# A mixture-of-experts kernel behind attention: units of 512 tokens in place of units of 256

## The chip, the cores and the metric

The kernel runs on one core of one Trainium2 chip. The metric is the device time of one execution in microseconds (us). Engines are named as the profile names them: PE is TensorE (PEld its weight loads), DVE is VectorE, ACT is ScalarE, POOL is GpSimd and SP is SyncE, which only issues transfers here.

## What is computed

The reference is sparse attention followed by a top-1 mixture of experts. Attention has 4 batches, 8 heads, 768 positions and 64 columns a head; a position sees the 96 before it and 8 global ones, with a linear bias on distance. Its rows (3072 x 512) go through a gate, and each token through the one expert that wins:

```python
    logits = x @ w_gate + modality_bias[modality_id]
    e_idx = np.argmax(logits, axis=1)
    # probs: softmax of logits; gate_w: the winner's probability
    for e in range(E):                                  # E = 8
        mask = e_idx == e
        h = np.maximum(x[mask] @ w1[e], 0.0)            # 512 -> 1024
        out[mask] = gate_w[mask, None] * (h @ w2[e])    # 1024 -> 512
```

How many tokens an expert gets is known only on the chip. With the inputs that are timed, experts 0, 3 and 5 get 1567, 1406 and 99 tokens, the others none.

## The kernel before

**Attention** is 24 steps of 128 rows, issued by `step(n)`: scores of block n on PE (L209), a maximum per row on DVE (L224, `mx`), exponentials on ACT (L240), four transposes for each of three PSUM banks (`t_mm`, L254), a copy of each bank to SBUF (`t_cp`), and the product with the values for block n - 2 (`pv`, L279 and L290). `t_cp(n, x, act)` puts a copy on ACT (L261) or on DVE (L263); the middle one of the three is DVE's, except in the last step. Behind the values come the row sums' reciprocal, the scaled rows (`xr`, L321), their transposes and copy (L335, L337), and the gate. When all six blocks of a batch have their gates, tokens are ranked by expert: matmuls `pk` (L409, L410) count them, a DVE copy (L419) takes the counts, and a scatter writes token numbers to `ids_sorted`. For three of the four batches that falls into steps 10, 16 and 22.

**Experts** follow, and three early units begin while the last batch is still ranked: 256 tokens each, of experts that the first two batches have filled (e0, e1, e2). Everything else waits for a plan that DVE works out on the chip in arrays of expert by item (`items`, `slots`, `granules`): 8 units of 256 (s0 to s7) and granules of up to 128 tokens (g0, g1), the last a small one of up to 32 rows beside the final unit (g2). The order of the slots is e0, e1, e2, s0, s1, g0, s2, s3, g1, s4 to s7. The plan's instructions come from a generator, `rest()`, that `fill(u, k)` advances once for each of 16 parts of an early unit; so they stand between that unit's own instructions on DVE.

A slot loads 4 MB of weights. fp32 accuracy comes from splitting each operand into a high part, cast by ACT (L665 for weights, L680 for tokens), and the rest, subtracted by DVE (L666, L681), and from three matmuls for each product. `l1_unit` has weights stationary and 256 tokens moving: 96 matmuls of 256 columns (L694 to L696), two of the eight feature blocks in one PSUM bank, then ReLU on ACT (L700) and the subtraction on DVE (L701) 512 wide. `l2` has tokens stationary: 48 matmuls of 512 columns (L736 to L738), into one bank `po` for each 128 tokens. `fin` scales a bank into SBUF on ACT (L805) and POOL scatters the rows (L806). `x_t` transposes the next slot's tokens late in a slot, four transposes and one ACT and one DVE instruction for each 128 tokens.

**What sets the order.** PE and ACT run in the order that the program writes. The scheduler interleaves DVE's instructions. SP works in order, and a load of token numbers or weights first reads a register from the plan's result. Each `po` comes from a pool of two banks, so a bank must be emptied by ACT before it is filled again.

## Time and profile before

| what | value |
|---|---|
| runs | 448.81, 448.84, 450.58 us; median 448.84 us |
| profiled execution | 451.22 us, of which the span on the core is 449.3 us |
| busy | PE 429.9 us (96%), DVE 300.9 (67%), ACT 274.5 (61%), POOL 111.4 (25%) |
| mean granted TensorE clock | 0.992 of full speed |
| bytes moved | 110.24 MB at a mean of 245 GB/s |
| attention | from the first scores at 5.4 us until about 143 us |
| experts | from there to about 437.7 us, PE busy throughout |

Busy time counts from an instruction's start to its end, and matmuls overlap, so the distance between the starts of two is what a matmul costs in a full stream. "Idle before <- releaser" in a row names what ended a wait. The rest of the span, from 437.7 to 449.3 us, is the last scatter and its landing.

### The profile page before, as it was taken

How to read it: one execution, taken by the hardware profiler on the slowest of the kernel's cores; microseconds unless marked ns; L12 is line 12 of the kernel's file. 1: busy time of each engine (PE TensorE's matmuls, PEld its weight loads, DVE VectorE, ACT ScalarE, POOL GpSimd, SP SyncE). 2: the span in 40 equal slices, each digit the busy share in tenths (PEclk: the TensorE clock that was granted, in tenths of full speed). 3: DMA queues.
4: the chain of work that ended last, by engine and by line, in shares of the span. 5: the costliest groups of instructions: out<-in, count | busy, mean ns of one | idle time of the engine just before them, and what ended most of it. 6: DMA issues, size and time to landing. Idle time of an engine off the chain costs nothing.

```text
span 449.3 us, 12795 instructions
## 1 busy us (share of the span) xinstructions
PE 429.9 (96%) x4872; PEld 378.8 (84%) x4872; DVE 300.9 (67%) x945; ACT 274.5 (61%) x508; POOL 111.4 (25%) x173
## 2 busy tenths in 40 slices
PE   7999998989999999999999999999999999999990
PEld 7889887878887989889898988989889898989860
DVE  7878786778778678898374786574956746465500
ACT  5988887877877263645554677454864645554420
POOL 6010013122423257340404053021123030301010
PEclk9999999999999999999999999999999999999996
DMA  8999999987867658485848488675797666565510
GB/s 238 323 332 329 343 366 332 276 249 249 290 214 251 231 174 348 154 288 204 306 157 302 165 310 303 231 258 210 242 364 255 226 229 215 185 211 208 187 34 27
DMA packets 58197, 110.24 MB, mean 245 GB/s; under 512 B 8575, under 2 KB 22399, under 8 KB 58128
## 3 DMA queue, kind: packets, MB, share of 16 engines
q1 hardware_dynamic: 53456, 96.49, 64.4%
q0 software_dynamic: 4672, 12.85, 7.8%
q8 instruction: 40, 0.66, 0.6%
q14 instruction: 29, 0.24, 0.1%
HBM read 94.95 MB, written 14.43 MB: 243 GB/s over the span
## 4 chain that ended last, share of the span: by engine, by line
PE 75%; issue 13%; DVE 3%; ACT 3%; DMA 2%; POOL 2%; POOLq 0%; SPq 0%; DVEq 0%; ACTq 0%
PE s L209 6%; PE pt L254 6%; PE phs L696 5%; PE phs L694 5%; PE phs L695 5%; PE x L290 5%; PE pos L738 4%; PE pos L737 4%; PE pos L736 4%; PE phe L694 3%; PE phe L696 3%; PE phe L695 3%; PE poe L738 2%; PE poe L736 2%; PE poe L737 2%
## 5 line engine op out<-in xcount | busy, mean ns | idle before, releaser
L240 ACT ACTIVATE pr<-sc,nmx 128x168 f32<-128x168 f32 x192 | 67.6, 425 | 13.3 <-DVE nmx L224 10.7
L696 PE MATMUL phs<-xhs,als 128*128 128x256 f32 x256 | 72.4, 283 | 0.0
L694 PE MATMUL phs<-xhs,ahs 128*128 128x256 f32 x256 | 72.3, 282 | 0.0
L695 PE MATMUL phs<-xls,ahs 128*128 128x256 f32 x256 | 72.2, 282 | 0.0
L224 DVE CUSTOM_DVE_ANT_0 sc<-s,tbl 128x168 f32<-128x168 f32 x192 | 52.7, 329 | 15.0 <-PE s L209 13.4
L701 DVE SCALAR_TENSOR_TENSOR hls<-phs,hhs 128x512 fp32r<-128x512 f32 x32 | 22.1, 692 | 51.1 <-ACT hhs L700 48.5
L618 POOL DMA_INDIRECT xgs<-x_rows,uis x16 | 24.0, 1501 | 119.6 <-DMA uis<-ids_sorted 56.7
L736 PE MATMUL pos<-bhs,hhs 128*128 128x512 f32 x128 | 52.0, 406 | 0.0
L738 PE MATMUL pos<-bhs,hls 128*128 128x512 f32 x128 | 50.6, 396 | 0.0
L737 PE MATMUL pos<-bls,hhs 128*128 128x512 f32 x128 | 50.5, 394 | 0.0
L694 PEld LDWEIGHTS phs<-xhs,ahs 128*128 128x128 f32 x256 | 48.9, 191 | 0.4
L700 ACT ACTIVATE hhs<-phs 128x512 fp32r<-128x512 f32 x32 | 19.1, 598 | 49.2 <-PE phs L696 38.5
L695 PEld LDWEIGHTS phs<-xls,ahs 128*128 128x128 f32 x256 | 48.9, 191 | 0.3
L696 PEld LDWEIGHTS phs<-xhs,als 128*128 128x128 f32 x256 | 48.9, 191 | 0.1
L209 PE MATMUL s<-kt,qt 64*64 64x168 f32 x768 | 38.0, 312 | 2.7 <-DVE nmx L224 1.9
L445 POOL DMA_INDIRECT ids_sorted<-tki,pi x24 | 26.5, 1103 | 43.6 <-ACT pr L240 31.0
L254 PE MATMUL pt<-ident,pr 128*128 128x128 f32 x288 | 36.7, 277 | 0.0
L209 PEld LDWEIGHTS s<-kt,qt 64*64 64x64 f32 x768 | 29.6, 132 | 7.5 <-DVE nmx L224 3.7
L254 PEld LDWEIGHTS pt<-ident,pr 128*128 128x128 f32 x288 | 31.0, 141 | 4.5 <-issue 3.2
L261 ACT COPY pT<-pt 128x512 f32<-128x512 f32 x49 | 28.3, 587 | 6.7 <-PE pt L254 5.0
L736 PEld LDWEIGHTS pos<-bhs,hhs 128*128 128x128 f32 x128 | 24.1, 189 | 6.7 <-issue 2.1
L806 POOL DMA_INDIRECT out<-obs,ois x16 | 16.6, 1037 | 52.7 <-ACT obs L805 50.2
(346 smaller groups left out, 999.9 us busy)
## 6 DMA issues: line engine op xcount, KB each, us to landing
va<-in_vr SPq DMA_DIRECT2D x24, 520.0 KB
kt<-in_ks SPq DMA_DIRECT2D x24, 272.0 KB
qt<-in_qs SPq DMA_DIRECT2D x24, 256.0 KB
x_rows<-xr SPq DMA_DIRECT2D x24, 256.0 KB
vl<-in_vo SPq DMA_DIRECT2D x48, 81.2 KB
rawe0a<-in_moe_w SPq DMA_DIRECT2D x4, 512.0 KB
rawe0b<-in_moe_w SPq DMA_DIRECT2D x4, 512.0 KB
rawe1a<-in_moe_w SPq DMA_DIRECT2D x4, 512.0 KB
```

Source lines behind the costliest of these rows:

```text
L209: nc.tensor.matmul(ps[g][64 * half : 64 * half + 64, c0 : c0 + W], qt[hs, hp, 64 * half : 64 * half + 64], kt[hs, hp, w0 : w0 + W], start= ...
L224: V.tensor_tensor_reduce(out=sc, in0=pss[n][g][:, c0 : c0 + W], in1=(tbl0 if n % NB == 0 else tbl)[:, hh, :], op0=ALU.add, op1=ALU.min, sc ...
L240: last[0] = nc.scalar.activation(pr[:, h * (PRW - W) : h * (PRW - W) + W], scs.pop((n, hh)), AF.Exp, bias=blk[n][:, hh : hh + 1], scale=-1.0,)
L254: nc.tensor.transpose(tp[:, j * P : (j + 1) * P], prs[(NP * n + hp) % NPR][:, o : o + P], ident)
L261: last[0] = nc.scalar.copy(pT.rearrange("p a b -> p (a b)"), tp)
L445: ins = nc.gpsimd.indirect_dma_start(out=ids, out_offset=bass.IndirectOffsetOnAxis(ap=pi[:, j : j + 1], axis=0), in_=tki[:, b * NB + j, :] ...
L694: nc.tensor.matmul(o, hi[:, fs], s.xh[:, c, :], start=(c == 0), stop=False)
L695: nc.tensor.matmul(o, hi[:, fs], s.xl[:, c, :], start=False, stop=False)
L696: nc.tensor.matmul(o, lo[:, fs], s.xh[:, c, :], start=False, stop=(c == 3))
L736: nc.tensor.matmul(s.po[t], s.hh[:, fc, tt], hi[:, wv], start=(fc == 0), stop=False)
L737: nc.tensor.matmul(s.po[t], s.hh[:, fc, tt], lo[:, wv], start=False, stop=False)
L738: nc.tensor.matmul(s.po[t], s.hl[:, fc, tt], hi[:, wv], start=False, stop=(fc == 7))
```

## The change

The tokens that the early units leave are taken in three *duos* of 512 tokens (`halves` = 4, named b0 to b2), two units of 256 (c0, c1) and the same granules. With the inputs that are timed the plan makes duos of (expert 0, tokens 768 to 1279), (3, 0 to 511) and (3, 512 to 1023), units of (0, 1280 to 1535) and (3, 1024 to 1279), and granules of 126, 99 and 31 tokens, which are the tokens of the 8 units and 3 granules before. The order is e0, e1, e2, b0, g0, b1, g1, c0, b2, c1, with g2 beside the last. There are 11 slots that load weights where there were 14.

- `l1_duo` makes one PSUM bank from a feature block and 512 moving tokens: 96 matmuls, and two ReLUs and two subtractions 256 wide for each of the 8 blocks.
- The second layer of a duo is two passes over the same weights, tokens 0 to 255 and then 256 to 511. Between them `fin(s, [0, 1])` empties the two banks.
- The plan sorts items into duos, odd units and rests. `granules` looks at four thresholds in place of two, over 32 places in place of 16, and the generator is advanced twice for a part of an early unit, except in the first unit's first parts.
- The split b weights have one buffer in place of two. A duo's further tiles come from a new pool, `mp2`. A granule's b split is written at parts 17, 19, 21 and 23 of a duo. Transposes of the next slot's tokens are up to four.
- In the attention, `t_cp` of the middle bank goes to ACT in three more steps: 10, 16 and 17.

```diff
@@ -35,13 +35,14 @@
 U = 256
 NE = 3
 BE = 2
-NS = 8
+ND = 3
+NS = 5
 NGR = 3
 NGF = 2
 MR = 32
 NI = 17
-NR = NI - NS
-NGT = 16
+NR = NI - ND
+NGT = 32
...
-ORDER = (0, 1, 8, 2, 3, 9, 4, 5, 6, 7, 10)
-TX = (11, 12)
-TB = (7, 9, 11, 13)
+ORDER = (0, 5, 1, 6, 3, 2, 4, 7)
+TB = (17, 19, 21, 23)
...
+        units, full = pl("units", [E]), pl("full", [E])
         V.tensor_scalar(ci, ci, 8, None, ALU.logical_shift_right)
+        V.tensor_copy(units, ci)
+        V.tensor_scalar(ci, ci, 1, None, ALU.logical_shift_right)
         V.tensor_copy(full, ci)
+        odd = pl("odd", [E])
+        V.scalar_tensor_tensor(odd, full, -2.0, units, ALU.mult, ALU.add)
...
+        V.tensor_tensor(m3, bm(sin, ni), uc, ALU.is_gt)
+        V.tensor_tensor(w, bm(sex, ni), uc, ALU.is_gt)
+        V.tensor_sub(m3, m3, w)
+        V.tensor_tensor(w, m3, bm(full, ni), ALU.mult)
+        V.tensor_add(st, st, w)
...
-        h1 = pl("h1", [NR])
-        V.tensor_scalar(h1, nr, 0.0, None, ALU.is_gt)
-        h2 = pl("h2", [NR])
-        V.tensor_scalar(h2, nr, 128.0, None, ALU.is_gt)
-        m = pl("m", [1])
-        V.reduce_sum(m, h1, axis=AX.X)
-        m2 = pl("m2", [1])
-        V.reduce_sum(m2, h2, axis=AX.X)
...
+        lt = pl("lt", [NR, NR])
+        V.tensor_tensor(lt, bc(uidx[:, 0:NR], NR), bm(uidx[:, 0:NR], NR), ALU.is_gt)
+        m, m2 = pl("m", [1]), pl("m2", [1])
+        V.memset(m, 0.0)
+        sa, sk, wr, wk = pl("sa", [NGT, NR]), pl("sk", [NGT, NR]), pl("wr", [NGT]), pl("wk", [NGT])
+        hk, pk, w1_ = pl("hk", [NR]), pl("pk", [NR]), pl("w1", [NR, NR])
         gi = uidx[:, 0:NGT]
-        gm = pl("gm", [NGT])
-        V.tensor_scalar(gm, gi, m, None, ALU.subtract)
-        s1 = pl("s1", [NGT, NR])
-        behind(V.tensor_tensor(s1, bc(gi, NR), bm(uidx[:, 0:NR], NGT), ALU.is_equal), last[0])
-        V.tensor_tensor(s1, s1, bm(h1, NGT), ALU.mult)
-        s2 = pl("s2", [NGT, NR])
-        V.tensor_tensor(s2, bc(gm, NR), bm(uidx[:, 0:NR], NGT), ALU.is_equal)
-        V.tensor_tensor(s2, s2, bm(h2, NGT), ALU.mult)
         yield
+        for k in range(4):
+            V.tensor_scalar(hk, nr, 128.0 * k, None, ALU.is_gt)
+            V.tensor_tensor(w1_, lt, bm(hk, NR), ALU.mult)
+            V.reduce_sum(pk, w1_, axis=AX.X)
+            V.tensor_scalar(pk, pk, m, 1.0, ALU.add, ALU.add)
...
+            t = sk if k else sa
+            V.tensor_tensor(t, bc(gi, NR), bm(pk, NGT), ALU.is_equal)
+            if k:
+                V.reduce_sum(wk, sk, axis=AX.X)
+                if k == 1:
+                    V.tensor_copy(wr, wk)
+                else:
+                    V.scalar_tensor_tensor(wr, wk, float(k), wr, ALU.mult, ALU.add)
+                V.tensor_add(sa, sa, sk)
...
-        nb = 2 if which == "b" and s.straight else 1
         pool = wspb if which == "b" or early else wsp
-        th = pool.tile([P, 1024], F32R, tag=f"{which}h{c}{early}", name=f"{which}h{s.name}{c}", bufs=nb)
-        tl = pool.tile([P, 1024], F32R, tag=f"{which}l{c}{early}", name=f"{which}l{s.name}{c}", bufs=nb)
+        th = pool.tile([P, 1024], F32R, tag=f"{which}h{c}{early}", name=f"{which}h{s.name}{c}", bufs=1)
+        tl = pool.tile([P, 1024], F32R, tag=f"{which}l{c}{early}", name=f"{which}l{s.name}{c}", bufs=1)
...
+            pool, w = (mp2, 2 * U) if s.halves == 4 else (mp, U)
+            s.xh = pool.tile([P, 4, w], F32R, tag="xh", name=f"xh{s.name}")
+            s.xl = pool.tile([P, 4, w], F32R, tag="xl", name=f"xl{s.name}")
...
+        if s.halves == 4:
+            s.hh2 = mp2.tile([P, 8, U], F32R, tag="hh", name=f"hh{s.name}b")
+            s.hl2 = mp2.tile([P, 8, U], F32R, tag="hl", name=f"hl{s.name}b")
+
+    def l1_duo(s, f):
+        ph = p_t(f"ph{s.name}{f}")
+        fs = slice(f * P, (f + 1) * P)
+        for c in range(4):
+            hi, lo = s.hi["a", c], s.lo["a", c]
+            nc.tensor.matmul(ph, hi[:, fs], s.xh[:, c, :], start=(c == 0), stop=False)
+            nc.tensor.matmul(ph, hi[:, fs], s.xl[:, c, :], start=False, stop=False)
+            nc.tensor.matmul(ph, lo[:, fs], s.xh[:, c, :], start=False, stop=(c == 3))
+        for hh, hl, o in ((s.hh, s.hl, 0), (s.hh2, s.hl2, U)):
+            last[0] = nc.scalar.activation(hh[:, f, :], ph[:, o : o + U], AF.Relu)
+            V.scalar_tensor_tensor(
+                hl[:, f, :], ph[:, o : o + U], 0.0, hh[:, f, :].bitcast(F32), ALU.max, ALU.subtract
+            )
...
-        if fc == 0 and not s.po:
-            s.po = {t: p_x(f"po{s.name}{t}") for t in range(2)}
+        if fc == 0 and t not in s.po:
+            s.po[t] = p_x(f"po{s.name}{t}")
         hi, lo = s.hi["b", fc // 2], s.lo["b", fc // 2]
         wv = slice(fc % 2 * 512, fc % 2 * 512 + 512)
-        tt = slice(t * P, (t + 1) * P)
-        nc.tensor.matmul(s.po[t], s.hh[:, fc, tt], hi[:, wv], start=(fc == 0), stop=False)
-        nc.tensor.matmul(s.po[t], s.hh[:, fc, tt], lo[:, wv], start=False, stop=False)
-        nc.tensor.matmul(s.po[t], s.hl[:, fc, tt], hi[:, wv], start=False, stop=(fc == 7))
+        tt = slice(t % 2 * P, (t % 2 + 1) * P)
+        hh, hl = (s.hh2, s.hl2) if t > 1 else (s.hh, s.hl)
+        nc.tensor.matmul(s.po[t], hh[:, fc, tt], hi[:, wv], start=(fc == 0), stop=False)
+        nc.tensor.matmul(s.po[t], hh[:, fc, tt], lo[:, wv], start=False, stop=False)
+        nc.tensor.matmul(s.po[t], hl[:, fc, tt], hi[:, wv], start=False, stop=(fc == 7))
...
-            t_cp(n - 1, 1, n == LAST)
+            t_cp(n - 1, 1, n in (NB + 4, 2 * NB + 4, LAST - 1, LAST))
...
-        uei, uoi, inv = slots("b", plan, *[t[:, 0:NS] for t in r], NS, 2)
-        for u in range(NS):
-            slist.append(mk(f"s{u}", uei[0:1, u : u + 1], uoi[0:1, u : u + 1], inv[:, :, u], xd, 2))
-        yield
+        for tag, u0, u1, hv in (("b", 0, ND, 4), ("c", ND, NS, 2)):
+            uei, uoi, inv = slots(tag, plan, *[t[:, u0:u1] for t in r], u1 - u0, hv)
+            for u in range(u1 - u0):
+                slist.append(mk(f"{tag}{u}", uei[0:1, u : u + 1], uoi[0:1, u : u + 1], inv[:, :, u], xd, hv))
+            yield
...
+    mp2 = sM.enter_context(tc.tile_pool(name="mp2", bufs=1, side="right", reuse_waits="tile"))
     man = tc.manual_schedule(engines={ET.Activation})
     man.__enter__()
     bg = rest()
@@ -1394,6 +1436,8 @@
         s = order[u]
         if u < NE:
             next(bg, None)
+            if u or k > 8:
+                next(bg, None)
...
-        if nx.halves == 1 and k in TB:
+        if nx.halves == 1 and s.halves == 4 and k in TB:
             split(nx, "b", TB.index(k))
-        if k >= 8 and k % 2 == 0:
+        if 8 <= k < 16 and k % 2 == 0:
             if ("a", k // 2 - 4) in nx.raw:
                 split(nx, "a", k // 2 - 4)
-        if s.halves == 2 and k in TX:
-            x_t(nx, TX.index(k))
+        if s.halves > 1:
+            x0 = (23 if s.halves == 4 else 15) - 2 - max(nx.halves, 2)
+            if x0 <= k < x0 + nx.halves:
+                x_t(nx, k - x0)
...
-        for m in range(0 if u else LF, 16):
-            if m >= 8:
+        for m in range(0 if u else LF, 24 if s.halves == 4 else 16):
+            if m >= 8 and s.halves == 4:
+                for t in (0, 1):
+                    l2(s, (m - 8) % 8, m // 16 * 2 + t)
+                if m == 15:
+                    fin(s, [0, 1])
...
+            elif s.halves == 4:
+                l1_duo(s, m)
...
-            if s.halves == 1 and m in (7, 10) and u + 1 < nslot:
-                x_t(order[u + 1], m // 10)
-        if u + 1 < nslot:
+            if s.halves == 1 and m in (7, 9, 10, 12) and u + 1 < nslot:
+                ts = (7, 10) if order[u + 1].halves == 2 else (7, 9, 10, 12)
+                if m in ts:
+                    x_t(order[u + 1], ts.index(m))
+        if s.halves == 4:
+            fin(s, [2, 3])
```

The listing of instructions in each engine's order shows three places. The first is on PE at the end of the second layer. `pos` and `pob` are the PSUM banks `po` of a unit and of a duo, `hhs` and `hhb` the hidden activations, `bhs` and `bhb` the b weights, `phs` the next slot's first layer. Before, at the end of the first unit of the plan:

```order
L736 MATMUL pos_4821<-bhs_4816,hhs_4656 128x512
L737 MATMUL pos_4821<-bls_4817,hhs_4656 128x512
L738 MATMUL pos_4821<-bhs_4816,hls_4657 128x512
L694 MATMUL phs_4916<-xhs_4854,ahs_4828 128x256 [waits Activation_49]
L695 MATMUL phs_4916<-xls_4855,ahs_4828 128x256 [waits DVE_49]
L696 MATMUL phs_4916<-xhs_4854,als_4829 128x256
```

Now, between the two passes of the first duo:

```order
L776 MATMUL pob_4950<-bhb_4942,hhb_4748 128x512
L777 MATMUL pob_4950<-blb_4943,hhb_4748 128x512
L778 MATMUL pob_4950<-bhb_4942,hlb_4749 128x512
L776 MATMUL pob_5024<-bhb_4828,hhb0b 128x512 [waits Activation_49]
L777 MATMUL pob_5024<-blb_4829,hhb0b 128x512
L778 MATMUL pob_5024<-bhb_4828,hlb0b 128x512
L776 MATMUL pob_5028<-bhb_4828,hhb0b 128x512 [waits Activation_49]
```

A unit's second layer is followed by the next slot's first layer, which writes other banks; a duo's first pass is followed by matmuls that write the pool's two banks again, each with a wait on ACT.

The second place is the step with the ranking matmuls of the second batch (step 16): `pT` is the copy of the middle bank, `xr` the scaled rows, `pks` the counts. On DVE:

```order
 L321 TENSOR_TENSOR xr_2337<-x_0_2278,rin_2333 128x4x64
 L321 TENSOR_TENSOR xr_2337<-x_1_2279,rin_2333 128x4x64
-L263 COPY pT_1_2353<-pt_1_2348 128x512
 L419 COPY pks_2374<-pk_2371 128x96
 L224 ISA sc_7_2409,nmx_2408<-s_2_2395,tbl 128x168
```

and on ACT in the same step:

```order
 L346 COPY lps_0_2318<-s_2_2236 128x128
 L261 COPY pT_0_2346<-pt_0_2341 128x512
+L261 COPY pT_1_2353<-pt_1_2348 128x512
 L261 COPY pT_2_2360<-pt_2_2355 128x512
 L337 COPY xT_1_2367<-tx_1_2362 128x512
```

The copy leaves DVE's queue ahead of the counts and stands on ACT between the two others. Steps 10 and 17 have the same pair.

The third place is on DVE ahead of the third early unit: `ale` is the rest of its a weights, `xle` of its tokens, names with g are the granules' plan and names with b and c the units'. Before:

```order
L681 TENSOR_TENSOR xle_4269<-mte_4270,xhe_4268 128x4x128 [waits Activation_49]
L564 TENSOR_SCALAR ggm<-uidx,gm 128x16 [waits DVE_49]
L666 TENSOR_TENSOR ale_4333<-rawe2a_3807,ahe_4332 128x1024 [waits DMAHW6_49,Activation_49]
L569 TENSOR_TENSOR gs_4230<-ggm,uidx 128x144 [waits DVE_49]
L581 TENSOR_TENSOR gm<-gm,gm_4223 128x1
L681 TENSOR_TENSOR xle_4269<-mte_4336,xhe_4268 128x4x128 [waits Activation_49]
L570 TENSOR_TENSOR gs_4230<-gs_4230,gh_4219 128x144 [waits DVE_49]
L666 TENSOR_TENSOR ale_4380<-rawe2a_3809,ahe_4379 128x1024 [waits DMAHW7_49,Activation_49]
```

Now, the end of the same stretch:

```order
L543 SCALAR_TENSOR_TENSOR uofc<-uexb,ustb 128x2
L547 TENSOR_SCALAR invc<-ustb,pidx 128x2
L549 TENSOR_SCALAR invc<-ustb,pidx 128x2
L687 TENSOR_TENSOR ale_4436<-rawe2a_3810,ahe_4435 128x1024 [waits DMAHW6_49,Activation_49]
L545 CAST uoib<-uofb 128x3 [waits DVE_49]
L703 TENSOR_TENSOR xle_4421<-mte_4439,xhe_4420 128x4x128 [waits Activation_49]
L550 TENSOR_TENSOR invb<-invb,ulib 128x12 [waits DVE_49]
L545 CAST uoic<-uofc 128x2 [waits DVE_49]
L550 TENSOR_TENSOR invc<-invc,ulib 128x4 [waits DVE_49]
L563 TENSOR_SCALAR ustb<-ustb 128x2
L687 TENSOR_TENSOR ale_4459<-rawe2a_3812,ahe_4458 128x1024 [waits DMAHW7_49,Activation_49]
```

Where the granules' plan stood, the units' plan stands now; the granules' comes behind the last of these subtractions.

## Rows read from the trace of the kernel before

Rows of a timeline give start us, length us, engine, line, operation, result and operands, shape and count, and in brackets the idle time before it and what ended it.

**Rows 1.** The page's first part: each engine's busy time, share and instructions.

```profile
PE 429.9 (96%) x4872; PEld 378.8 (84%) x4872; DVE 300.9 (67%) x945; ACT 274.5 (61%) x508; POOL 111.4 (25%) x173
```

**Rows 2.** Table by stretches of the span, of core 0.

```profile
core 0: us, PE busy (x) PEld busy (x) DVE busy (x) ACT busy (x) POOL busy (x), PEclk, DMA share, GB/s
97.00:102.40 5.40, 5.40 (x129) 4.84 (x128) 4.51 (x32) 3.94 (x11) 2.98 (x11) 1.00 0.67 188
172.00:197.00 25.00, 25.00 (x162) 22.54 (x161) 20.86 (x71) 13.69 (x18) 11.92 (x12) 1.00 0.68 240
197.00:220.00 23.00, 23.00 (x148) 20.71 (x148) 18.35 (x51) 11.69 (x16) 6.13 (x5) 1.00 0.75 245
220.00:240.00 20.00, 20.00 (x138) 18.46 (x138) 11.46 (x13) 10.94 (x15) 2.18 (x3) 1.00 0.66 228
240.00:437.70 197.70, 197.70 (x1247) 172.71 (x1246) 115.06 (x124) 108.59 (x142) 41.63 (x32) 1.00 0.66 229
```

**Rows 3.** Timeline of PE, start of a unit's first and second layer.

```profile
start us, us, engine line op out<-in xcount [idle before <-releaser]
303.08 0.28 PE L694 MATMUL phs<-xhs,ahs 128*128 128x256 f32 x1
...
314.58 0.39 PE L736 MATMUL pos<-bhs,hhs 128*128 128x512 f32 x1
...
315.28 0.40 PE L736 MATMUL pos<-bhs,hhs 128*128 128x512 f32 x1
```

**Rows 4.** Timeline of PE and ACT at a unit's end.

```profile
242.66 0.40 PE L738 MATMUL pos<-bhs,hls 128*128 128x512 f32 x1
...
243.60 0.28 PE L694 MATMUL phs<-xhs,ahs 128*128 128x256 f32 x1
...
243.15 1.39 ACT L805 ACTIVATE obs<-pos,uis 128x512 f32<-128x512 f32 x2 [2.00 <-issue]
```

**Rows 5.** Groups by line and shape, from 172 us on.

```profile
line engine op names shapes xcount | busy us, mean ns | idle before us <-releasers
L700 ACT ACTIVATE hhs<-phs 128x512 fp32r<-128x512 f32 x32 | 19.1, 598 | 49.2 <-PE phs L696 38.5 <-issue 10.6
...
L681 DVE TENSOR_TENSOR xls<-mts,xhs 128x512 fp32r<-128x512 f32 x16 | 11.0, 688 | 4.1 <-ACT xhs L680 4.0
...
L666 DVE TENSOR_TENSOR bls<-raws0b,bhs 128x1024 fp32r<-128x1024 f32 x4 | 4.9, 1225 | 1.0 <-ACT bhs L665 1.0
...
L480 DVE TENSOR_TENSOR cexb<-cinb,fullb 128x8 f32<-128x8 f32 x1 | 0.2, 167 | 0.0
```

**Rows 6.** Timeline of PE, DVE and ACT in step 16.

```profile
96.80 0.18 PE L409 MATMUL pk<-oh,tri 128*128 128x48 bf16 x1 [1.58 <-DVE pT L263]
...
96.06 0.68 DVE L263 COPY pT<-pt 128x512 f32<-128x512 f32 x1
97.04 0.26 DVE L419 COPY pks<-pk 128x96 f32<-128x96 f32 x1 [0.30 <-PE pk L410]
97.59 0.33 DVE L224 CUSTOM_DVE_ANT_0 sc<-s,tbl 128x168 f32<-128x168 f32 x1 [0.29 <-PE s L209]
...
90.75 2.98 ACT L240 ACTIVATE pr<-sc,nmx 128x168 f32<-128x168 f32 x8 [0.32 <-DVE nmx L224]
...
97.97 0.44 ACT L240 ACTIVATE pr<-sc,nmx 128x168 f32<-128x168 f32 x1 [1.96 <-DVE nmx L224]
```

**Rows 7.** Timeline of PE and DVE in step 18.

```profile
104.21 0.36 PE L209 MATMUL s<-kt,qt 64*64 64x168 f32 x2 [0.48 <-DVE nmx L224]
...
103.23 0.68 DVE L263 COPY pT<-pt 128x512 f32<-128x512 f32 x1
```

**Rows 8.** Timeline of PE, DVE and ACT, start of the third early unit.

```profile
196.24 0.28 PE L694 MATMUL phe<-xhe,ahe 128*128 128x256 f32 x1
...
197.71 0.39 PE L696 MATMUL phe<-xhe,ale 128*128 128x256 f32 x1
...
196.45 1.21 DVE L666 TENSOR_TENSOR ale<-rawe2a,ahe 128x1024 fp32r<-128x1024 f32 x1
...
192.25 0.59 ACT L680 CAST xhe<-mte 128x512 fp32r<-128x512 f32 x1 [0.30 <-PE mte L677]
```

**Rows 9.** Timeline of PE at the start of the attention.

```profile
8.40 1.58 PE L209 MATMUL s<-kt,qt 64*64 64x168 f32 x32 [1.38 <-DVE nmx L224]
```

**Rows 10.** Waits in step 10: us in total, times, longest us.

```profile
PE pk L409 <- ACT pT L261: 0.2, 1, 0.2
```

More of the change, by code (lines that the diff above doesn't have):

```diff
@@ L491, in items @@
         yield
+        V.tensor_tensor(m3, bm(sin, ni), uc, ALU.is_gt)
[3 more added lines that the diff above has]
+        V.tensor_add(st, st, w)
+        yield
         rem = pl("rem", [E])
-        V.scalar_tensor_tensor(rem, full, -float(U), left, ALU.mult, ALU.add)
+        V.scalar_tensor_tensor(rem, units, -float(U), left, ALU.mult, ALU.add)
         key = pl("key", [E])
@@ L537, in slots @@
         V.tensor_scalar(inv[:, 0, :], ust, pidx, None, ALU.add)
-        if halves == 2:
-            V.tensor_scalar(inv[:, 1, :], ust, pidx, 128.0, ALU.add, ALU.add)
+        for h in range(1, halves):
+            V.tensor_scalar(inv[:, h, :], ust, pidx, 128.0 * h, ALU.add, ALU.add)
         V.tensor_tensor(inv, inv, bm(uli, halves), ALU.is_ge)
@@ L549, in pl @@
             return plan.tile([P] + shape, dt, name=f"g{name}")
-        iex, ist, ili = uex[:, NS:NI], ust[:, NS:NI], uli[:, NS:NI]
+        iex, ist, ili = uex[:, ND:NI], ust[:, ND:NI], uli[:, ND:NI]
+        one = slice(0, NS - ND)
+        V.tensor_scalar(ist[:, one], ist[:, one], float(U), None, ALU.add)
         nr = pl("nr", [NR])
         V.tensor_sub(nr, ili, ist)
-        h1 = pl("h1", [NR])
-        V.tensor_scalar(h1, nr, 0.0, None, ALU.is_gt)
-        h2 = pl("h2", [NR])
-        V.tensor_scalar(h2, nr, 128.0, None, ALU.is_gt)
```

91 lines of the change are left out of this document (49 added, 42 removed).

## The prediction

> **What bounds the kernel now.** I read the page first. TensorE (PE) is busy 96% of the span [rows 1], so a microsecond is worth something only if PE loses it or PE computes for it. The table by stretches comes next [rows 2]: from 172 to 437.7 us PE is busy all of the time at a granted clock of 1.00, the 2.4 GHz level, while DVE has 25.00 - 20.86 = 4.1 us free before 197, 4.7 us from there to 220 and 8.5 us in the 20 us behind. The expert stage is therefore bound by the number of matmuls times their spacing, with DVE as the engine that could come up beside it. Third, the rows of PE in time. In one unit's first layer the first matmul of 256 columns starts at 303.08 and the second layer at 314.58 [rows 3]: 96 matmuls in 11.50 us, 119.8 ns each. In the second layer 512 columns follow each other at (315.28 - 314.58) / 3 = 0.233 us [rows 3]. I use those spacings and not the 0.28 or 0.39 us that a row gives for one matmul, since the records overlap. Fourth, the waits: in the attention stage PE does lose time, and the rows where it does are [rows 6, 7, 9, 10].
>
> **The change part by part.**
>
> *First layer with 512 columns.* A duo issues 96 matmuls of 512 where two units issue 2 x 96 of 256. At the second layer's spacing that is 96 x 0.233 = 22.3 us against 2 x 11.50 = 23.0, so -0.7 us for a duo and -2.1 for three. Bounds: 0.233 is read from matmuls whose moving operand is a weight, here it is tokens; if the spacing were exactly twice 119.8 ns, the term is 0, and below 0.23 no row of 512 columns goes. I take -2.1: the nearest row has the same width and the same type.
>
> The Trainium skill speaks to this place (page "TensorE: Matmul & The Clock Gate", section "Back-to-back issue gap"): it gives a sustained spacing of about 131 ns for 512 columns. By it a duo's first layer would take 12.6 us and the three would save some 31 us, as an estimate from that page. The trace has 233 ns in this kernel's own fp32r stream, so the measurement decides, and the rule is left a hundredth as the fourth rival.
>
> The ReLU and the subtraction behind it become two of 256 columns for each of the 8 blocks. One of 512 is 598 ns on ACT, and DVE's subtraction of that width 688 [rows 5]; two blocks of a unit are one such pair. The count of columns is the same, the count of instructions doubles. Even at the 512-wide price for each, ACT would need 2 x 0.6 = 1.2 and DVE 1.4 us for a block of 12 x 0.233 = 2.8 us. PE hides both: 0.
>
> *Second layer in two passes.* The order, as the section on the change shows it, puts the second pass right behind the first, on the same two banks, and its first matmul waits for ACT. Its cost is in the trace of a unit's end: the last matmul of the first bank starts at 242.66, ACT starts the two evictions at 243.15 and takes 1.39 us for both, 0.69 each [rows 4]. The first bank is free at 243.84; PE would have been ready at 243.60, where the next slot's first layer now starts without waiting. That is 0.24 us; with the time that the semaphore takes and the start behind a gap, which no row shows for this place, I take 0.35. The second bank is free at 244.54 and is asked for three matmuls (0.70) after the first, so it adds nothing. Bounds: 0.2, if the hand-over is free, and 0.7, if the first pass waits for a whole eviction. Three duos: +1.05 us (+0.6 to +2.1). The tail of each pass and the last eviction of a duo are as at a unit's end.
>
> *Fewer weight slots.* 14 slots of 4 MB become 11: 24 casts and 24 subtractions of 1.22 us [rows 5] go, 29 us of DVE spread over the stage. PE never waits there [rows 2], so 0. In the other direction, the b halves get one buffer in place of two: their casts are issued in the slot's own first layer, when the previous second layer is over, so nothing waits that did not. Four transposed blocks ahead of a duo in place of two cost ACT 0.59 [rows 8] and DVE 0.69 us [rows 5] more apiece; a duo needs its last a chunk only at its tenth matmul, 9 x 0.233 = 2.1 us in, where a unit asks for it after 1.1. I count 0.
>
> *The plan.* By the listing DVE issues 146 planning instructions where it issued 86. Ten are 128x448 and four 128x196; the trace has 128x8 at 167 ns and 128x512 at 688 [rows 5], so I estimate 0.62 and 0.35 us by the line through those two. The rest are short ones, of whose 167 ns I count 0.12, since their starts overlap. Together 6.2 + 1.4 + 45 x 0.12 = about 13 us more. All of it runs from 172 us on, where the stretches of rows 2 leave 4.1 + 4.7 + 8.5 = 17.3 us free. It hides if it comes in the right order. Two places need that.
>
> At the third early unit, the trace has 1.47 us for its first eleven matmuls (196.24 to 197.71) where eleven times 0.12 is 1.32: PE waits 0.15 us for DVE's last subtraction, which starts at 196.45 [rows 8]. The order shows the granules' part gone from between those subtractions and the units' part in its place, about as many short ones. The block's copy on ACT starts at 192.25 and is 0.59 us [rows 8]; from 192.84 on, DVE's two subtractions of a block, two of a chunk (1.22) and some 12 short ones make 0.6 + 0.6 + 1.13 + 1.21 + 12 x 0.13 = 5.1 us, an end at 197.9 against 196.24 + 1.32 = 197.6 wanted. So between a gain of 0.15 and a loss of 0.6; I take 0.
>
> At the first duo, four a chunks must be subtracted before about 222.8 us (the plan's first unit starts at 220, the edge of a stretch of rows 2; two more transposed blocks on PE are about 0.7, and the tenth matmul is 2.1 us in). Counting the instructions in DVE's order at these prices, I come to 220.1 for the last. A margin of 2.7 us: 0.
>
> *Copies moved.* One PSUM copy in each of steps 10, 16 and 17 goes from DVE to ACT. In step 16 PE waits 1.58 us for that copy (96.06, 0.68 us, behind the row sums) before the ranking matmuls at 96.80 [rows 6]. Without it PE could start at about 95.3. But DVE is next: its next score pass starts at 97.59, and it has 0.68 of copy and 0.30 + 0.29 us of waiting to give before it [rows 6]. So 1.27, not 1.58. One step on, PE waits 0.48 us for a score maximum which stands behind the copy at 103.23 [rows 7]; 0.68 us of copy goes there, of which I take 0.6. In step 10 PE waits 0.2 us for a copy [rows 10]; I take 0.3 with what the DVE is freed of. ACT gets 0.59 us in each of these steps, but waits there for DVE up to 1.96 us [rows 6], which covers it. Sum -2.2 us; bounds -0.8, if ACT's third copy only moves the wait, and -2.7, if all that PE waits goes.
>
> *The start.* One 128x196 instruction now stands on DVE ahead of the table's last operation; ACT waits for that, then DVE, then PE, which starts the second block of scores at 8.40 after waiting 1.38 us [rows 9]. +0.25 us, between 0.1 and 0.35.
>
> **Sum**: -2.1 + 1.05 + 0 - 2.2 + 0.25 = -3.0 us. The profiled execution took 451.22 us (449.3 of span and 1.9 around it), so 448.2 in the same terms. The median of the runs shown, 448.84, is 2.4 us below the profiled one; the terms are differences, so I predict 445.8.
>
> **Rivals.**
> 1. *The copies move the wait.* In a step with three copies ACT has 2.98 us of exponentials [rows 6] and four copies of 0.59, 5.3 us before its smaller instructions; such a step lasts 5.4 us where only PE counts (a row of the table by stretches: 97.00 to 102.40, all of it PE) [rows 2]. If ACT becomes late, the gain of 2.2 falls to 0.8, and PE's second pass may wait nearer 0.7: -2.1 + 2.1 - 0.8 + 0.25 = -0.55, 448.3. For it: that sum. Against: the three steps aren't neighbours of other heavy ones on ACT, which waits 1.96 us there.
> 2. *Slower: DVE becomes the bound at the first duo.* Place: its a chunks' subtractions behind the plan. Price: if the added instructions cost 18 us, half-way between my 13 and 24 (every wide one at 0.69 and each short one at 0.3), and all stand ahead of them, 18 - 8.8 free before 220 - 2.7 of margin = 6.5 us of PE idle; 445.8 + 6.5 = 452.3. It decides from the moment the last of them ends behind 222.8. For it: DVE is 80 to 83% busy there [rows 2] and PE already waits for DVE at 197.7 [rows 8]. Against: the 128x448 ones mostly stand behind the duo's splits.
> 3. *The clock falls.* In the duo's first layer one bank is filled after another with gaps only if ACT and DVE are late; PE's granted clock was 1.00 through second layers that do the same [rows 2]. The Trainium skill's page "TensorE: Matmul & The Clock Gate" (section "A second HAM failure mode: psum-queue depth-cycling") tells of a 512-column kernel that cycled through banks and lost the full clock again and again. If one duo's first layer ran at the 1.2 GHz level, PE would need 22.3 us more, 468. The trace speaks against it.
> 4. *512 columns cost no more than 256.* If a matmul of the duo's first layer came every 119.8 ns, as one of 256 does, three duos would save 34.5 us and not 2.1: 413. No row of 512 columns speaks for it. The rule on the gap, named above, points this way.
>
> **Chances.** My forecast, with its own range of 444.2 to 446.9: 0.58. The first rival (446.9 to 450): 0.26. The second (450 to 455): 0.13. The third 0.02, the fourth 0.01. About 0.5%, 2.2 us, is what a measurement can tell, so faster means under 446.6, slower over 451.1. Faster: 0.58 less a tenth of it, plus a little of the first rival: 0.58. Same: 0.30. Slower: 0.12. For the range I take 443.4, where every bound of the terms is at its good end (-2.1 + 0.6 - 0.15 - 2.7 + 0.1 = -4.25, 444.6, and a microsecond more for what the trace doesn't show), to 449.6.
>
> **What would show it.** Duo: the distance from its first to its second layer is 22.3 us, at 233 ns a matmul; 23.0 would make that term 0. Pass boundary: a gap of 0.35 us on PE before the ninth block of the second layer, ended by ACT's eviction. Copies: the step with the ranking matmuls no longer waits 1.58 us; if the gap is still there with an ACT copy or the score maximum as its cause, rival 1. Plan: no idle time of PE between 190 and 225 with DVE as its cause; if there is, rival 2. The forecast is wrong if PE's idle time in the expert stage exceeds 2 us, or if the attention stage ends later than 1 us before where it ends now.

## The result and the profile after

The changed kernel takes 443.5 us (median of 12 runs, 442.7 to 447.4), the kernel before 449.46 us beside it (12 runs): a ratio of 0.986 with a 95% interval of 0.9835 to 0.9885, some 6 us less. Two later comparisons on other chips gave 0.9846 (0.9798 to 0.9894) and 0.9861 (0.981 to 0.9912). The prediction had 3.0 us.

The profiled execution has a span of 441.8 us against 449.3. Its first part, to be held against [rows 1]:

```profile
PE 426.5 (97%) x4584; PEld 363.5 (82%) x4584; DVE 287.7 (65%) x1000; ACT 256.8 (58%) x511; POOL 104.4 (24%) x173
```

The table by stretches, to be held against [rows 2]:

```profile
172.00:197.00 25.00, 25.00 (x167) 22.83 (x166) 22.95 (x69) 13.47 (x18) 9.19 (x10) 1.00 0.52 163
197.00:220.00 23.00, 23.00 (x136) 20.11 (x135) 21.63 (x48) 12.51 (x17) 6.34 (x5) 1.00 0.58 216
220.00:240.00 20.00, 20.00 (x89) 16.42 (x88) 15.04 (x54) 8.93 (x19) 2.91 (x3) 1.00 0.55 193
```

DVE's free time before 220 us went from 8.8 to 3.4 us (25.00 - 22.95 and 23.00 - 21.63 are left of the two stretches); PE stays busy throughout at a granted clock of 1.00, the 2.4 GHz level.

The ends of stages say where the time went. E0 is the start of the first expert's first layer, and the expert stage is counted from there to the start of the last unit's first layer; all are starts of PE rows in each kernel's timeline.

| profile | E0, us | expert stage, us |
|---|---|---|
| before | 146.65 | 262.90 |
| before, second profile | 144.35 | 264.24 |
| changed | 142.32 | 259.77 |
| changed, second and third | 142.51, 142.78 | 259.62, 259.60 |

The expert stage of the changed kernel is the same each time and 3.1 to 4.6 us shorter, where 1.05 was forecast (-2.1 + 1.05). E0 scatters by more than that: the first two profiles differ by 4.3, the pair on one chip by 1.84 (144.35 and 142.51), where 1.95 was forecast (-2.2 + 0.25).

PE, at the first duo's first layer, at its second layer and at the boundary between the passes, the places of [rows 3, 4] (the cuts are marked with dots):

```profile
216.23 0.39 PE L717 MATMUL phb<-xhb,ahb 128*128 128x512 f32 x1
...
238.20 0.39 PE L776 MATMUL pob<-bhb,hhb 128*128 128x512 f32 x1
...
248.96 0.40 PE L778 MATMUL pob<-bhb,hlb 128*128 128x512 f32 x1
249.49 0.51 PE L776 MATMUL pob<-bhb,hhb0b 128*128 128x512 f32 x1
249.83 0.40 PE L777 MATMUL pob<-blb,hhb0b 128*128 128x512 f32 x1
```

The first layer is 21.97 us, 228.9 ns a matmul; the second and third duo's are 22.36 and 21.97. At the boundary the first two matmuls of the second pass start 0.53 and 0.34 us after the one ahead of them, where 0.23 is the spacing: 0.40 us lost, as forecast (0.35). Yet a duo's whole second layer is not longer than two units'. It takes 22.80 us with one block of four transposes in it; a unit's takes 12.05 with two such blocks and 12.82 with four, so each block adds 0.38. Without the blocks it is 22.4 us for the duo against 22.6 for two units.

Step 16, against [rows 6], PE and then DVE:

```profile
94.92 0.19 PE L409 MATMUL pk<-oh,tri 128*128 128x48 bf16 x1
```

```profile
94.69 0.76 DVE L321 TENSOR_TENSOR xr<-x,rin 128x256 f32<-128x256 f32 x2
95.37 0.25 DVE L419 COPY pks<-pk 128x96 f32<-128x96 f32 x1
95.72 0.33 DVE L224 CUSTOM_DVE_ANT_0 sc<-s,tbl 128x168 f32<-128x168 f32 x1
```

The ranking matmuls wait for nothing, and DVE goes from the scaled rows to the counts and on to its score pass with at most 0.10 us between two of them (95.37 + 0.25 to 95.72). The step takes 5.48 us where it took 7.22.

### The profile page after: what moved, and what is told of

It is laid out like the page before. It is cut to its first block, busy times and chain, and to the rows that moved or that the text cites. A ratio compares the mean times of both kernels' runs of the same rounds, so it can differ in the third digit from the quotient of the medians.

```text
span 441.8 us, 12144 instructions
## 1 busy us (share of the span) xinstructions
PE 426.5 (97%) x4584; PEld 363.5 (82%) x4584; DVE 287.7 (65%) x1000; ACT 256.8 (58%) x511; POOL 104.4 (24%) x173
## 4 chain that ended last, share of the span: by engine, by line
PE 71%; issue 18%; POOL 3%; ACT 2%; DVE 2%; DMA 1%; POOLq 0%; SPq 0%
PE pt L254 7%; PE s L209 7%; PE x L290 6%; PE phb L718 3%; PE phb L719 3%; PE phb L717 3%; PE x L279 3%; PE pob L776 3%; PE tx L335 3%; PE phe L733 3%; PE pob L777 3%; PE pob L778 3%; PE phe L735 3%; PE phe L734 3%; PE poe L776 3%
## 5 line engine op out<-in xcount | busy, mean ns | idle before, releaser
L719 PE MATMUL phb<-xhb,alb 128*128 128x512 f32 x96 | 37.8, 393 | 0.0
L718 PE MATMUL phb<-xlb,ahb 128*128 128x512 f32 x96 | 37.6, 392 | 0.0
L717 PE MATMUL phb<-xhb,ahb 128*128 128x512 f32 x96 | 37.6, 391 | 0.0
L290 PE MATMUL x<-va,pT 128*64 128x65 f32 x768 | 27.7, 224 | 0.0
L733 PE MATMUL phe<-xhe,ahe 128*128 128x256 f32 x96 | 27.5, 287 | 0.0
L734 PE MATMUL phe<-xle,ahe 128*128 128x256 f32 x96 | 27.2, 283 | 0.0
L735 PE MATMUL phe<-xhe,ale 128*128 128x256 f32 x96 | 27.2, 283 | 0.0
L290 PEld LDWEIGHTS x<-va,pT 128*64 128x64 f32 x768 | 24.4, 137 | 1.6
L718 PEld LDWEIGHTS phb<-xlb,ahb 128*128 128x128 f32 x96 | 18.0, 188 | 4.5 <-DVE xlb L703 0.4
L719 PEld LDWEIGHTS phb<-xhb,alb 128*128 128x128 f32 x96 | 18.0, 188 | 3.9
```

What stands on the lines that cost most here:

```text
L290: nc.tensor.matmul(px[h][64 * half : 64 * half + 64, hp * D1 : (hp + 1) * D1], pT_of(n, hp, 2 * h)[:, 64 * half : 64 * half + 64], va[r][: ...
L717: nc.tensor.matmul(ph, hi[:, fs], s.xh[:, c, :], start=(c == 0), stop=False)
L718: nc.tensor.matmul(ph, hi[:, fs], s.xl[:, c, :], start=False, stop=False)
L719: nc.tensor.matmul(ph, lo[:, fs], s.xh[:, c, :], start=False, stop=(c == 3))
L733: nc.tensor.matmul(o, hi[:, fs], s.xh[:, c, :], start=(c == 0), stop=False)
L734: nc.tensor.matmul(o, hi[:, fs], s.xl[:, c, :], start=False, stop=False)
```

## The experiments

Each run's ratio is its time to that of the kernel before, run beside it on the same chip, with a 95% interval.

**The three copies, undone and alone.** The first edit is in the changed kernel; the second run has the reverse in the kernel before:

```diff
-            t_cp(n - 1, 1, n in (NB + 4, 2 * NB + 4, LAST - 1, LAST))
+            t_cp(n - 1, 1, n == LAST)
```

> The changed kernel with the three middle copies (steps 10, 16 and 17) put back on DVE; all else as changed. Theory A (the copies are worth more than the 2.2 us of the prediction, because each wait that they cause also delays the step behind it): 3 to 4 us slower than the changed kernel, about 447, and the steps 10, 16 and 18 are long again (5.9, 7.2, 6.8 us against 5.4 to 5.7). Theory B (the copies are worth what was reckoned, and the surplus of the attention comes from PE gaps that nothing in the program causes and that lie elsewhere in each run): 2.2 us slower, about 445.7, and the profile shows one or two gaps of about 1 us put down to issue, in some other step.

> The kernel before with only the three copies moved to ACT. Theory A: 3 to 4 us faster than before, 445.5 to 446.5. Theory B: 2.2 us faster, about 447.2. In both the steps 10, 16 and 18 shrink to 5.4 to 5.7 us; if ACT's third copy moved the wait (the prediction's first rival) they shrink by less than 0.8 in all.

(`LAST` is 18 of the 24 steps, so step 18 has that copy on ACT in both kernels; the description of the kernel before wrongly has "the last step".)

Ratios to before: 0.9898 (0.9868 to 0.9928) and 0.9988 (0.9948 to 1.0028). The steps 10, 16 and 18 are long with the copies on DVE (5.85, 7.22, 6.74 us) and 5.48, 5.48 and 6.30 with them on ACT, but step 19 becomes 6.31 in the second. Both profiles also have PE gaps of 0.2 to 1.4 us in steps 2, 12 and 18 and in the last that are put down to issue, that is, to no wait that the profile shows. In the time the copies alone gave 0.5 us, less than either theory had, while the three steps shrank by 2.6 against the profile with the copies on DVE. That speaks for theory B, with intervals too wide to divide anything.

**The width of the first layer.**

```diff
-        for c in range(4):
-            nc.tensor.matmul(ph, hi[:, fs], s.xh[:, c, :], ...)   # and two more
+        for o in (slice(0, U), slice(U, 2 * U)):
+            for c in range(4):
+                nc.tensor.matmul(ph[:, o], hi[:, fs], s.xh[:, c, o], ...)   # and two more
```

> The changed kernel with each matmul of a duo's first layer cut in two of 256 columns into the halves of the same bank; the slots, the plan, the two passes and the copies stay. If the 512 columns carry the gain of the expert stage: the first layer takes 23.0 us again in place of 22.0 to 22.4 (read from the changed kernel's trace), 2.7 us for three duos, about 446.2; the prediction's own term was 2.1. Rival: the first layer's width is worth nothing and the gain comes from the fewer slots: no difference beyond 0.5 us.

Ratio 0.9873 (0.9814 to 0.9931). The first layers take 22.62, 22.42 and 22.62 us, 1.4 to 1.5 us more for the three than in the changed kernel's profiles. So the width gives some 1.5 of the 2.6 us by which first layers got shorter; the rest comes without it, since 256 columns here follow each other in 117.8 ns and in most units in 119.8. By the times alone this run is not apart from the changed kernel.

**The boundary.** `fin(s, [1, 0])` in place of `fin(s, [0, 1])`.

> The changed kernel with the two evictions between a duo's passes in the other order, so that the bank which the second pass wants first is emptied last. If PE waits for exactly that eviction, as the prediction has it (0.24 us and more at a boundary): one eviction of 0.69 us more at each of three boundaries, 2.1 us slower, about 445.6, and PE shows a gap of 0.8 to 1.0 us there. Rival: the boundary costs nothing since something else hides it: under 0.5 us.

Ratio 0.9907 (0.9872 to 0.9943), expert stage 261.79 us: 2.0 to 2.2 more than in the changed kernel's three profiles, where 2.1 was expected.

```profile
253.59 0.40 PE L778 MATMUL pob<-bhb,hlb 128*128 128x512 f32 x1
254.82 0.50 PE L776 MATMUL pob<-bhb,hhb0b 128*128 128x512 f32 x1 [0.83 <-ACT obb L845]
```

With that eviction made the second of the two, the second pass starts 1.23 us after the last matmul of the first in place of 0.53. PE waits for exactly the first bank's eviction: the mechanism was read rightly.

**Both kernels again, the planning instruction held back, the plan made heavier.** The edits are `behind(V.tensor_tensor(lt, ...), last[0])`, and `for _ in range(5):` around the comparison that makes `t` in `granules`.

> The changed kernel once more, beside the others of this call: the ratio to before that the mechanisms must add up to. If the gain of about 6 us belongs to the program, the ratio is again 0.984 to 0.989. If a part of it was PE gaps put down to issue, which fell otherwise in the first profile, the ratio moves towards 0.990 and the profile shows gaps of about 1 us in steps 2, 12, 13 or in the tail of the attention, while from the first expert's first layer to the last unit's it takes 259.8 us again.

> The kernel before once more, for a second profile. What the program causes is there again: steps 10, 16 and 18 of 5.9, 7.2 and 6.8 us, and 262.9 us from the first expert's first layer to the last unit's. The 6.8 us of step 12, which nothing in the change touches, should be there again if the program causes it (theory A) and be otherwise if it is a gap of instruction supply (theory B).

> The changed kernel with the one planning instruction of 128x196 held back, so that it no longer stands in DVE's queue ahead of the bias table. The prediction gave it 0.25 us; the changed kernel's trace has the first step 0.4 to 0.7 us later by step 4 than before, apart from a gap put down to issue. So 0.3 to 0.7 us faster than the changed kernel in the trace up to step 4, which the times can hardly tell; rival: no difference, since the first steps wait for transfers anyway.

> The changed kernel with each of the plan's four 128x448 comparisons made five times, 16 instructions of 0.62 us more on DVE between the second early unit and the first duo, of which some seven stand ahead of the duo's last subtraction. In the changed kernel that subtraction ends at 216.1 us and PE wants it at 218.3, a margin of 2.2 us. If the margin is as read: the subtraction ends at about 219.5, PE waits 1 to 1.5 us for DVE at the duo's start, and the rest hides; about 1 us slower than the changed kernel. If the plan's load is hidden in full whatever its size (the scheduler puts it into idle time): no wait. If DVE is the bound there: 5 us or more.

The changed kernel's ratio was 0.9846 again. The second profile of before has steps 10 and 18 (5.86, 6.21) and 16 (6.65) long again, but step 12 of 5.44 us: the 6.78 of the first profile is not there each time, so the program alone does not cause it. And it lost PE time at a place that looked clean in the first:

```profile
276.36 0.16 DVE L796 TENSOR_TENSOR oig<-uig,invg 128x1 int32<-128x1 int32 x1 [1.70 <-DMA uig<-ids_sorted]
276.43 0.68 DVE L681 TENSOR_TENSOR xls<-mts,xhs 128x512 fp32r<-128x512 f32 x1
277.03 2.35 DVE L666 TENSOR_TENSOR als<-raws2a,ahs 128x1024 fp32r<-128x1024 f32 x2
```

```profile
278.65 0.28 PE L695 MATMUL phs<-xls,ahs 128*128 128x256 f32 x1
279.44 0.39 PE L696 MATMUL phs<-xhs,als 128*128 128x256 f32 x1 [0.51 <-DVE als L666]
```

This is the unit behind the first granule. DVE's tiny addition for the rows of the *second* granule stands between that unit's subtractions and waits 1.70 us for the transfer of the token numbers; then PE waits for the last subtraction. PE's first layer takes 12.63 us there and 11.85 behind the second granule, where it needs 11.35 without such a wait (the kernel with the row numbers held back, below). Of the 1.27 us lost, the rows show 0.51 as idle time: the matmuls' records overlap, so busy time hides short waits.

Holding the planning instruction back changed nothing that shows: ratio 0.9869 (0.9823 to 0.9916), step 4 starts at 23.91 us against 23.62 to 24.10, and DVE's first score pass at 6.42 against 6.39 (6.12 in the kernel before).

The heavier plan took 453.2 us, ratio 1.0051 (1.002 to 1.0083): more than any theory had, and by none of the mechanisms expected. PE does not wait at the first duo's start (its first layer is 21.98 us). It waits at the boundary between the duo's passes:

```profile
250.40 1.05 ACT L687 CAST ahg<-rawg0a 128x1024 fp32r<-128x1024 f32 x1 [8.31 <-DMA rawg0a<-in_moe_w]
...
256.78 1.04 ACT L687 CAST ahg<-rawg0a 128x1024 fp32r<-128x1024 f32 x1 [1.29 <-DMA rawg0a<-in_moe_w]
257.73 1.26 ACT L846 ACTIVATE obb<-pob,uib 128x512 f32<-128x512 f32 x2
```

```profile
258.47 0.80 PE L777 MATMUL pob<-bhb,hhb0b 128*128 128x512 f32 x1 [7.63 <-ACT obb L846]
```

The plan's last results are the granule's token address. SP, in order, waits for it and has the granule's weights behind it: their load goes out at 246.38 us, in the changed kernel at 228.75. ACT, in order too, waits with the casts of those weights, and the eviction that PE wants stands behind them. The granted clock fell to 0.50, the 1.2 GHz level, while PE stood still, and was 1.00 again in the last of these stretches:

```profile
236.00:250.00 14.00, 14.00 (x63) 11.47 (x62) 10.42 (x43) 3.07 (x6) 1.95 (x2) 1.00 0.20 59
255.00:264.00 9.00, 5.53 (x13) 4.43 (x14) 2.45 (x2) 2.71 (x4) 2.29 (x2) 0.50 1.04 393
265.00:268.00 3.00, 3.00 (x17) 2.47 (x16) 1.29 (x2) 1.03 (x2) 0.31 (x1) 1.00 1.01 399
```

The duo's second layer is 33.06 us in place of 22.80: 7.6 of waiting and 2.6 from the first matmuls behind it, which at that clock follow each other in 427 ns. In the changed kernel the casts start at 240.50, 12 us behind the load, and wait for nothing.

**The wait for row numbers, taken away.** The first edit makes the addition dependent on the latest ACT instruction when a slot's rows are written out, so that it stands at the slot's end. The second, in the changed kernel, moves the first transposed block into the boundary between the passes. The four runs have the first edit in the kernel before, the second edit in the changed kernel, both in the changed kernel, and the first edit with the three copies on ACT in the kernel before.

```diff
-        V.tensor_tensor(s.oi[:, 0 : s.halves], s.ui[:, 0 : s.halves, 0], s.inv, ALU.add)
+        behind(V.tensor_tensor(s.oi[:, 0 : s.halves], ...), after)   # after = last[0], from fin
...
+            if s.halves == 4 and k == 15:
+                x_t(nx, 0)
```

> The kernel before, with DVE's small addition that makes a slot's output row numbers held back to the slot's own end. In the kernel before, that of the second granule stands in DVE's queue between the third plan unit's weight subtractions, and waits there for the transfer of its token numbers: 0.58 us in the first profile, 1.70 in the second, where PE then lost 1.1 us at the start of that unit. If this hidden wait is what the first reckoning missed: no wait of DVE for token numbers at that place, the first layers of the units behind the granules take 11.4 to 11.5 us in each profile, 262.4 to 262.9 us from the first expert's first layer to the last unit's, and the time falls by 0 to 1.3 us, 0.6 in the middle. Rival: the subtractions are late by themselves and the wait moves to the cast or the weights: the stall of PE stays.

> The changed kernel with the first transposed block of the slot behind a duo moved from the middle of the second pass to the boundary between the passes, where PE has 0.30 us of idle time and a first matmul that is 0.10 us longer. If the boundary's cost is PE waiting for ACT, the four transposes (0.36 us) fit into it: the second layer of each duo takes 22.4 us in place of 22.8, 1.1 us less for three, about a quarter of a per cent, which the trace shows and the times hardly do. Rival: the transposes push the second pass back, since their copy stands behind the evictions or the start behind a gap costs the same again: no difference.

> The changed kernel with both: the row numbers held back to the slot's end, and the transposes at the boundary between the passes. If both act: 1.1 us from the boundaries and 0.3 us at the start of the second duo, where PE waits 0.26 us for DVE, so a ratio to before about 0.3 per cent under that of the changed kernel (0.986 and 0.985 so far): 0.982. Rival: no more than filling the gap alone.

> The kernel before with the three copies moved to ACT and the row numbers held back, so that only the duos, their plan and the missing slots are left of the change. If the duos are worth what the traces say (first layers 2.7, second layers and boundaries 0.3, third early unit 0.2 us): 3 us slower than the changed kernel and 2.5 to 3.5 us faster than before, ratio 0.992 to 0.994. If the duos were worth only the 1.05 us of the prediction: ratio 0.988.

Ratios: 0.9931 (0.9898 to 0.9964), 0.9827 (0.9785 to 0.9869), 0.9819 (0.9779 to 0.9859), 0.9924 (0.9891 to 0.9958). The wait is gone in the first and fourth: 262.47 and 262.46 us of expert stage. In the kernel before it was 262.90 and 264.24, and 264.53 with the copies alone, where DVE waited 1.95 us for the second granule's row numbers. The filled boundary is what it should be, 22.36 us for the first duo's second layer:

```profile
254.37 0.40 PE L778 MATMUL pob<-bhb,hlb 128*128 128x512 f32 x1
254.60 0.60 PE L699 MATMUL mtg<-ident,xgg 128*128 128x128 f32 x4
254.95 0.48 PE L776 MATMUL pob<-bhb,hhb0b 128*128 128x512 f32 x1
```

These two are below the changed kernel's three ratios, by 0.2 to 0.4%, with intervals that overlap: the best versions by the trace (1.3 us less for the three second layers), not shown by the times. Both lost 0.9 us at the third early unit, whose token rests came late on DVE. Holding the row numbers back did not cure that, nor the 0.4 us that the second duo's first layer takes beyond the others (22.36 us in both runs), which it had been expected to do in part.

**On one chip, side by side.** Four of these again, beside the kernel before:

> The changed kernel, beside the next three on one chip. Ratio to before 0.984 to 0.987. From the first expert's first layer to the last unit's 259.6 to 259.8 us.

> The kernel before with the row numbers held back, again. If the first ratio (0.993, 3.1 us) was right: 0.990 to 0.996. If only the 0.4 to 1.8 us that the traces show are to be had: 0.996 to 0.999.

> The same with the three copies on ACT. Against the run above it is the price of the copies. If they are worth 2.2 us as in the prediction: 0.5 per cent less than the run above. If gaps in PE's supply eat them, as the first pair has it (0.9931 and 0.9924): 0.1 per cent less.

> The changed kernel with the three copies on DVE again. Against the first run of this call it is the price of the copies within the changed kernel: 0.5 per cent more if they are worth 2.2 us, 0.1 if not. Against the kernel with the row numbers held back it is the price of the duos alone: 3 us (0.7 per cent less) by the traces, 1.05 (0.2 per cent) by the prediction.

| kernel, one chip | median us | ratio to before (interval) | E0 | expert stage |
|---|---|---|---|---|
| before | 451.52 | 1 | | |
| row numbers held back | 449.06 | 0.9947 (0.992 to 0.9975) | 144.35 | 262.46 |
| and copies on ACT | 445.89 | 0.9862 (0.9823 to 0.9901) | 142.21 | 262.46 |
| changed, copies on DVE | 446.50 | 0.9885 (0.9841 to 0.9929) | 144.66 | 259.79 |
| changed | 444.33 | 0.9861 (0.981 to 0.9912) | 142.78 | 259.60 |

The copies take 3.2 or 2.2 us off the median and 2.1 or 1.9 off E0. The duos take 1.6 or 2.6 off the median and 2.9 or 2.7 off the expert stage, less 0.3 to 0.6 at the start. The wait for row numbers is 2.5 us of the median. By the ratios (0.9862 and 0.9861) the units with copies on ACT and without the wait are level with the changed kernel, by the medians 1.6 us behind it: the times do not tell these two apart, the expert stage does.

The earlier pair, on another chip, is to be held beside this: the kernel with the row numbers held back, and the same with the copies on ACT. There, too, the copies make the steps 10, 16 and 18 shorter, 17.28 us together in place of 19.85 (here 16.62 in place of 18.73, and 16.64 in place of 18.73 with the duos). But there the median falls by 0.45 us only (452.64 to 452.19; ratios 0.9931 and 0.9924), and E0 comes 0.45 later: other steps are longer, step 12 by 1.2 and the last by 1.9 us, with 2.3 us of PE gaps put down to issue where the other profile has 0.7.

## Why the prediction was wrong

Most terms have the right sign (the second layer's has not), but the sum is 3 us short. Against units with the wait taken away the duos shorten the expert stage by 2.7 to 2.9 us where 1.05 was forecast: some 1.8 us, from the two layers' spacings. The rest of what was missed is a wait that the kernel before has and the prediction put at nothing. With the profiles' numbers the sum closes: -2.8 for the duos, -2.2 for the copies, +0.45 at the start and -0.4 to -2.1 for the wait make -5.0 to -6.7, and 6.0 was measured.

- **Copies: right in the steps.** -2.2 forecast; the steps 10, 16 and 18 are 2.1 to 2.6 us shorter in each of the three pairs, and no row of them has PE waiting for a copy on ACT, so rival 1 did not happen. How much of it reaches the time is less sure: 2.2 and 3.2 us on one chip, 0.45 on another, 0.5 by the ratio of the copies alone.
- **The start: the size by luck.** +0.25 forecast, 0.3 to 0.6 measured as the difference of E0 between kernels with and without the duos. But holding back the instruction that was blamed recovered nothing, so it is not the cause, which stays open.
- **"Fewer weight slots ... PE never waits there [rows 2], so 0": this is the step that failed.** It took from one profile's busy time that PE loses nothing from 172 to 437.7 us. But in the kernel before DVE's additions for row numbers, each waiting for a transfer, stand ahead of subtractions that PE needs soon. Three such places cost PE time: the third early unit and the units behind the two granules. In the profile that the prediction was made from, the first two of these waits are

```profile
193.03 0.16 DVE L796 TENSOR_TENSOR ois<-uis,invb 128x2 int32<-128x2 int32 x1 [0.98 <-DMA uis<-ids_sorted]
...
277.79 0.16 DVE L796 TENSOR_TENSOR oig<-uig,invg 128x1 int32<-128x1 int32 x1 [0.58 <-DMA uig<-ids_sorted]
```

They cost 0.26 us at the third early unit (11.76 us; 11.50 with the row numbers held back), where the prediction saw PE wait for DVE and put it down to short planning instructions, and 0.2 behind the granules. In the second profile of the kernel before, the places behind the granules cost 1.8 us; the wait at the third early unit is longer there, 2.17 us, but ends half a microsecond further ahead of the unit and costs nothing. In the profile with the copies alone the three cost 2.1. In the changed kernel the addition still waits, but further ahead of what PE needs: before the second duo it stands 5.8 us ahead of the first layer, which starts at 274.65.

```profile
268.85 0.16 DVE L836 TENSOR_TENSOR oic<-uic,invc 128x2 int32<-128x2 int32 x1 [1.52 <-DMA uic<-ids_sorted]
```

Taking the wait away alone gave 0.9931 and 0.9947, 3.1 and 2.4 us, with both intervals below 1. In the three profiles it is 0.4, 1.8 and 2.1 us of the expert stage; the two larger values lie within those intervals, the first does not. How often an execution pays which of them is not known.
- **Second layer in two passes: the wait right, but +1.05 is the other term that failed.** 0.40 us a boundary (forecast 0.35), but the whole came out at about -0.3 us and not +1.05 for three duos, since the other matmuls of the duo's second layer follow each other in 229 ns and a unit's in 232 to 235. The prediction counted what the boundary adds and took the spacing to stay.
- **First layer: mis-sized.** -2.6 us in place of -2.1: three duos and one unit have 77.6 to 77.8 us of first layer, seven units 80.2 with the row numbers held back. Some 1.5 of it is the width, the rest a closer spacing. The bound "below 0.23" did not hold: 0.229.
- **The plan: the margins right, the danger elsewhere.** The third early unit takes 11.52 us; that it took 11.76 in the first profile of the kernel before was the wait named above (11.50 in the second). The first duo's last subtraction ends at 216.08 us, 2.2 ahead of the tenth matmul, with which the prediction reckoned 2.7; the matmul that reads its result is the twelfth, 2.7 behind. But the price of a late plan is not there, as rival 2 had it: it is paid through SP's order and ACT's order at the boundary between the passes, and is 9 us with 16 instructions more.
- **The range:** its lower end should be 443.6 by its own sum (444.6 less a microsecond), not 443.4.
- The third and fourth rivals did not happen. The rule of the Trainium skill on the sustained spacing (page "TensorE: Matmul & The Clock Gate", section "Back-to-back issue gap") gives 131 ns for 512 columns; the changed kernel's rows have 229 ns in its first layer too, so the trace does not agree here.

What stays open: why the spacing differs between the same matmuls, what delays the start, and what causes the PE gaps put down to issue.

## What to carry to other kernels

A wait that costs nothing in one profile can cost microseconds in the next, when it is for a transfer and stands ahead of work with no slack. Look for small instructions that an in-order queue holds up for data which only something later needs, and count the slack behind them. A result that is late is paid for where the in-order queues meet, not where it is made: follow it through SP's loads and ACT's casts to the instruction of another slot that stands behind them. And a boundary at which PE waits for an eviction is a place for transposes that are due anyway.

## What the runs showed of the hardware that was not expected

The same 512-column matmul has several spacings that hold over whole stretches: 228.9 ns in the first and third duo's first layer, 230.3 in the second's behind a short wait, 229 in the duos' second layers and 232 to 235 in the units'. 256 columns have 119.8 in most units, 118.3 in the units behind a granule and 117.8 in the duos that were cut in halves. The granted clock is 1.00 in all of them. Some change at an interruption: in the first duo's second pass matmuls are 227 ns apart ahead of the transposed block, 225 to 236 in the dozen behind it, and then 227 again. The cause was not found.

PE stands still without a releaser in the attention, in pieces of 0.2 to 1.4 us, in all kernels and most often in steps 2, 12, 13, 18 and the last, while the 16 DMA engines are full (a share of 1.03 in the case shown). Together the pieces are 0.7 to 3.7 us in the profiles of the two chips on which the kernel before takes 454.5 and 456.3 us, and 0.2 to 1.9 on the two with 450.8 and 451.5. One case, of the kernel with swapped evictions:

```profile
74.42 0.31 PE L279 MATMUL x<-vl,pT 40*64 40x65 f32 x2 [0.42 <-issue]
75.24 0.31 PE L279 MATMUL x<-vl,pT 40*64 40x65 f32 x3 [0.51 <-issue]
75.97 0.33 PE L279 MATMUL x<-vl,pT 40*64 40x65 f32 x3 [0.43 <-issue]
```

Three transfers of the instruction queues fall into those three microseconds, but over all profiles such transfers do not go with the gaps: 36 of 69 gaps have none within 1.5 us of their middle, and the 69 have 44 in all where the mean rate of the attention would give 52. The cause is open.
